# A two-unit attention start rewritten: scores two tiles ahead, probabilities of the second unit scaled before their transposes, and a last tile in two buffers

## The chip, the cores and the metric

The kernel runs on one NeuronCore of one Trainium2 chip. The metric is the time of one execution in microseconds. Each time is measured on the device; the median of three runs is compared. A profile is one more execution, in which every engine's instructions are recorded: TensorE (PE, with its weight loads as PEld), VectorE (DVE), ScalarE (ACT), GpSimd (POOL) and SyncE (SP), whose queue issues nearly all transfers.

## The reference

Windowed attention with sink tokens, then a two-layer MLP without gating. Four batches, eight heads, 768 positions, head width 64; then 3072 tokens through 512 x 2048 and 2048 x 512 weights.

```python
scores = scale * np.matmul(q, k.transpose(0, 1, 3, 2))
is_sink = pos[None, :] < int(n_sink)                     # n_sink = 4
in_window = (rel >= 0) & (rel < int(window))             # window = 128
scores = np.where(is_sink | in_window, scores, -1000000000.0)
scores = scores - np.max(scores, axis=-1, keepdims=True)
a = np.exp(scores)
a = a / (np.sum(a, axis=-1, keepdims=True) + 1e-09)
x = np.matmul(a, v)                                      # then heads side by side: (3072, 512)
h = x @ w_in
out = np.maximum(0.01 * h, h) @ w_out
```

The weights arrive as 64-bit floats and are decoded on the chip.

## The kernel before

The 3072 tokens are cut into eight units of 384 (half a batch each, three tiles of 128 queries). For each unit the attention gives `x` transposed, 512 x 384, in four pieces of two heads (a pair). Each piece is split into a rounded part `xh` and the rest `xl`. The MLP of a unit goes through 16 blocks of 128 hidden columns: 12 matmuls give `h` (L559; four pieces, three products each), ACT multiplies by 0.01 (L566), DVE takes the maximum `g` (L567), ACT rounds it to `gh` (L568), `gl` is the rest (L569: POOL in unit 0, DVE later), and nine matmuls (L580) add to three output banks. The nine output matmuls of a block are issued after the `h` matmuls of the next one. There is one bank for `h`, so the next block's `h` waits until `g` has been taken.

While PE runs the MLP of unit u, the attention of the next unit is put between: `attention_stream` yields after each small step and `mlp_stream` after each group of matmuls, and the loop at the end of `fast_path` decides by counts (`early_steps`, `LEAD0`, `LEAD`) how many attention steps are due. On PE this is the order of issue (`manual_schedule`). The other engines' order is put together by a scheduler when the program is built; on the chip each engine then works through its own list in order.

Units 0 and 1 are special (`u < EARLY`). They are computed in full precision, two heads at a time (`attend_pair`). For each of three tiles: scores of two heads (L283), on DVE mask and row minimum of the negated scores (L303), on ACT the exponential with its row sum (L305); later the transposes of the probabilities (L354, L355) and their copy by ACT to `pt` (L357, L360). POOL copies the sink columns to `sk`. After the third tile `sinks` transposes `sk` (L386) and multiplies it by `diag` (L390), and spreads the reciprocal row sums over 384 columns with POOL (L395, `rs`). Then `values_pair` multiplies by the values (L412, L414), transposes `rs` (L418), copies it back by ACT (L419), and DVE multiplies the accumulated values by it (L421, `xf`); `emit_x` makes `xh` (ACT, L515) and `xl` (DVE, L516). Since `rs` is one number for each query and head, this divides by the row sum after the values. Steps that aren't due yet wait in the list `pend`: a tile's transposes come one score tile later.

Before PE's first score tile there are 22 warm-up matmuls on zeros (L604), and on DVE and POOL the masks (`build_masks`): `m0`, `m1`, `m2` for one head's tile and from them the two 260 columns wide ones of units 0 and 1 (L137, L139). Weights: `load_weights` fetches 512 KB (L152, L153), DVE decodes in three operations (L172, L174, L176), ACT rounds (L180), POOL gives the rest (L181). A fetch waits either for the decode four blocks back or for a softmax some steps back (`PRED`); four blocks are fetched in the early stage, the others in the MLP of unit 0. At the end each output bank goes through a buffer of the ring `io` (two buffers) to HBM (L593, L594); the last tile is copied in two halves by ACT and DVE (L588, L590) into one buffer of another ring, `wraw`, and stored by two queues.

Of the kernel before, what the change touches and what calls it, by code (L numbers as in the profile page):

```python
# [20 lines left out]
P = 128  # L21
# [23 lines left out]
LEAD0 = 5  # L45
# [9 lines left out]
WARM = 22  # L55
DEPTH = 4
PRE0 = 5
PRED = 7
# [5 lines left out]
def build_masks(nc, cpool, tpool, lims):  # L64
    raw = tpool.tile([P, 2, 2], I32, name="lim_raw")
    words = lims.bitcast(I32).rearrange("(o w) -> o w", o=1)
    nc.sync.dma_start(out=raw.rearrange("p i w -> p (i w)"), in_=words.broadcast_to([P, 4]))
    lo = tpool.tile([P, 2], F32, name="lim_lo")
    hi = tpool.tile([P, 2], F32, name="lim_hi")
    lim = cpool.tile([P, 2], F32, name="lim")  # L70
    nc.vector.tensor_copy(out=lo, in_=raw[:, :, 0])
# [4 lines left out]

    rel = tpool.tile([P, 2 * P], F32, name="rel")
    key = tpool.tile([P, P], F32, name="key")
    nc.gpsimd.iota(rel, pattern=[[-1, 2 * P]], base=P, channel_multiplier=1,
                   allow_small_or_imprecise_dtypes=True)  # L80
    nc.gpsimd.iota(key, pattern=[[1, P]], base=0, channel_multiplier=0,
                   allow_small_or_imprecise_dtypes=True)
    cur = tpool.tile([P, P], F32, name="cur")
    prv = tpool.tile([P, P], F32, name="prv")
    m0 = cpool.tile([P, P], F32, name="m0")
    m1 = cpool.tile([P, WM], F32, name="m1")
    m2 = cpool.tile([P, WM], F32, name="m2")
    tri = cpool.tile([P, P], I8, name="tri")
    nc.vector.tensor_scalar(out=cur, in0=rel[:, P:], scalar1=0.0, scalar2=None, op0=ALU.is_ge)
    nc.vector.tensor_scalar(out=tri, in0=rel[:, P:], scalar1=0.0, scalar2=None, op0=ALU.is_lt)  # L90
    nc.vector.scalar_tensor_tensor(out=cur, in0=rel[:, P:], scalar=win, in1=cur, op0=ALU.is_lt, op1=ALU.mult)
    nc.vector.scalar_tensor_tensor(out=m0, in0=key, scalar=ns, in1=cur, op0=ALU.is_lt, op1=ALU.max)
# [19 lines left out]
def fast_path(ctx, tc, cpool, qp, qk, vu, vs, w_in, w_out, out, ident, wz, lim, masks, tri, diag, negm, wmin, wmax):  # L112
# [21 lines left out]
    for n, m in enumerate(masks[1:]):  # L134
        e = apool.tile([P, W3], F32, tag="stg", name=f"wide{n}")
        for sign, base, dst in ((1, -1, e[:, 0:P]), (-1, 0, e[:, WM:])):
            nc.gpsimd.affine_select(out=dst, in_=m[:, NSK:], pattern=[[sign, P]], base=base,  # L137
                                    channel_multiplier=-sign, compare_op=ALU.is_ge, fill=-MASKED)
# [688 lines left out]
```

## Time and profile before

| | |
|---|---|
| three runs | 714.91, 713.47, 716.59 us; median 714.91 us |
| profiled execution | 712.43 us, its span 710.7 us, mean granted clock of PE 0.995 |
| first score matmul on PE | 6.25 us |
| first `h` matmul (L559) | 41.20 us |
| last matmul's end | 703.5 us |

The page gives the span, the busy shares of each engine and the chain that ended last. Other views answer questions on the trace: who waited for whom, groups of instructions with their mean duration, the rows of one engine in time, and a table by stages with busy times and granted clock. Times in them are from the start of the span. "[1.31 <-DVE g L567]" behind a row is the idle time of its engine before it, and what ended it. A wait for several things is put down to the last.

### The profile page before, as it was taken

What the parts mean: (1) busy time and instruction counts of PE and PEld (TensorE: products, weight loads), DVE (VectorE), ACT (ScalarE), POOL (GpSimd) and SP (SyncE); (2) the same over time, 40 slices, a digit from 0 to 9 for tenths busy, and PEclk for the clock granted to TensorE, in tenths of its full rate; (3) what the DMA queues carried; (4) which work ended last, traced back from release to release, by engine and by line L of the source; (5) the groups of instructions that cost most, each with busy time, mean ns of one, the idle gap of its engine ahead of it and who ended that gap; (6) DMA issues with size and microseconds to landing.
All of it is one profiled execution on the core that took longest, in us unless ns stands there. A gap on an engine that the chain in (4) does not pass through costs nothing.

```text
span 710.7 us, 12473 instructions
## 1 busy us (share of the span) xinstructions
PE 692.1 (97%) x3871; PEld 602.9 (85%) x3871; DVE 533.9 (75%) x1717; ACT 417.8 (59%) x1162; POOL 397.4 (56%) x536
## 2 busy tenths in 40 slices
PE   8799999999999999999999999999999999999995
PEld 4467778999899899998989799989899998999884
DVE  6788989666678888888889888888888978642222
ACT  5766666576656666666665676666667566422221
POOL 2346668555557777667666777748666665400000
PEclk9999999999999999999999999999999999999999
DMA  6756654221124342243324433334332310000001
GB/s 189 262 171 227 204 170 167 67 74 56 54 70 139 125 127 92 96 155 117 101 97 132 127 123 108 99 106 144 103 100 98 102 54 30 0 19 28 1 0 50
DMA packets 42603, 74.32 MB, mean 105 GB/s; under 512 B 3489, under 2 KB 26273, under 8 KB 42529
## 3 DMA queue, kind: packets, MB, share of 16 engines
q1 hardware_dynamic: 42384, 73.31, 32.0%
q8 instruction: 33, 0.54, 0.3%
q14 instruction: 42, 0.34, 0.2%
q10 hardware_dynamic: 144, 0.13, 0.1%
HBM read 67.14 MB, written 6.29 MB: 103 GB/s over the span
## 4 chain that ended last, share of the span: by engine, by line
PE 89%; DVE 5%; ACT 2%; DMA 1%; issue 1%; POOL 1%; POOLq 0%; ACTq 0%; DVEq 0%
PE h L559 36%; PE o L580 36%; PE v L439 5%; PE s L291 4%; PE t L365 2%; PE v L412 1%; PE s L283 1%; DMA wiraw<-in_w_in 1%; PE v L414 1%; DVE gl L569 1%; DMA woraw<-in_w_out 1%; PE t L386 0%; PE t L433 0%; PE t L355 0%; PE t L418 0%
## 5 line engine op out<-in xcount | busy, mean ns | idle before, releaser
L559 PE MATMUL h<-xh,wi 128*128 128x384 f32 x1024 | 311.3, 352 | 1.7 <-DVE g L567 1.3
L580 PE MATMUL o<-wo,gh 128*128 128x512 f32 x768 | 247.1, 403 | 0.0
L559 PEld LDWEIGHTS h<-xh,wi 128*128 128x128 f32 x1024 | 190.0, 188 | 16.7 <-issue 2.5
L559 PE MATMUL h<-xl,wi 128*128 128x384 f32 x512 | 172.8, 337 | 0.0
L335 POOL TENSOR_SCALAR_AFFINE_SELECT pt<-stg 128x256 fp32r<-128x256 f32 x240 | 105.3, 463 | 95.1 <-DVE stg L373 71.5
L580 PE MATMUL o<-wo,gl 128*128 128x512 f32 x384 | 151.4, 394 | 0.0
L580 PEld LDWEIGHTS o<-wo,gh 128*128 128x128 f32 x768 | 132.3, 189 | 17.2 <-issue 0.7
L567 DVE TENSOR_TENSOR g<-h,g 128x384 f32<-128x384 f32 x128 | 71.0, 555 | 64.0 <-ACT g L566 63.0
L566 ACT ACTIVATE g<-h 128x384 f32<-128x384 f32 x128 | 62.4, 487 | 70.1 <-PE h L559 68.8
L559 PEld LDWEIGHTS h<-xl,wi 128*128 128x128 f32 x512 | 96.9, 189 | 3.0
L580 PEld LDWEIGHTS o<-wo,gl 128*128 128x128 f32 x384 | 72.1, 188 | 17.9 <-DVE gl L569 0.2
L568 ACT CAST gh<-g 128x384 fp32r<-128x384 f32 x128 | 65.5, 511 | 35.1 <-DVE g L567 32.6
L569 DVE TENSOR_TENSOR gl<-g,gh 128x384 fp32r<-128x384 f32 x112 | 76.4, 682 | 11.5 <-ACT gh L568 9.9
L320 ACT ACTIVATE pk<-pk,negm 128x128 f32<-128x128 f32 (+1 forms) x144 | 58.1, 404 | 37.8 <-DVE negm L317 37.2
L242 POOL TENSOR_TENSOR qksp<-qkraw,qksp 64x392 fp32r<-64x392 f32 (+1 forms) x48 | 58.5, 1219 | 25.9 <-ACT qksp L241 18.0
L291 PEld LDWEIGHTS s<-qksp 128*128 128x128 f32 x288 | 53.2, 188 | 9.3 <-issue 2.9
L372 ACT CAST stg<-t 128x128 fp32r<-128x128 f32 x120 | 31.0, 258 | 47.9 <-PE t L365 34.0
L291 PE MATMUL s<-qksp 128*128 128x260 f32 (+1 forms) x288 | 56.3, 277 | 2.4 <-DVE negm L317 2.4
L244 POOL TENSOR_TENSOR qksp<-qkraw,qksp 128x384 fp32r<-128x384 f32 x48 | 51.9, 1082 | 3.8
L326 DVE TENSOR_SCALAR pk<-pk,sm 128x132 f32<-128x132 f32 (+1 forms) x120 | 47.5, 396 | 2.1
L439 PEld LDWEIGHTS v<-pt,vsp 128*128 128x128 f32 x336 | 45.1, 189 | 2.7 <-DVE xf L445 0.6
L241 ACT CAST qksp<-qkraw 128x776 fp32r<-128x776 f32 (+1 forms) x48 | 42.9, 893 | 6.7 <-PE s L291 3.4
(132 smaller groups left out, 1058.8 us busy)
## 6 DMA issues: line engine op xcount, KB each, us to landing
qkraw<-in_qk SPq DMA_DIRECT2D x24, 454.0 KB, 3.3
qkraw<-in_qk SPq DMA_DIRECT2D x24, 388.0 KB, 3.6
wiraw<-in_w_in SPq DMA_DIRECT2D x16, 512.0 KB, 3.8
woraw<-in_w_out SPq DMA_DIRECT2D x16, 512.0 KB, 3.8
ciraw<-in_w_in SPq DMA_DIRECT2D x16, 512.0 KB, 3.7
coraw<-in_w_out SPq DMA_DIRECT2D x16, 512.0 KB, 3.5
out<-ob SPq DMA_DIRECT2D x23, 256.0 KB, 2.0
vraw<-in_vu SPq DMA_DIRECT2D x14, 256.0 KB, 2.6
```

The costliest lines, as they stand in the source:

```text
L242: nc.gpsimd.tensor_tensor(out=sp[D:P, TU:TU + n], in0=raw[D:P, TU:TU + n], in1=sp[D:P, TU:TU + n].bitcast(F32), op=ALU.subtract)
L244: nc.gpsimd.tensor_tensor(out=sp[:, TU + n:2 * TU + n], in0=raw[:, 0:TU], in1=sp[:, 0:TU].bitcast(F32), op=ALU.subtract)
L291: nc.tensor.matmul(ps[:, 0:kn], lhsT=sp[:, off + j * P:off + (j + 1) * P], rhs=sp[:, TU + k0:TU + k0 + kn], start=c == 0, stop=c == len(pa ...
L320: nc.scalar.activation(out=w, in_=w, func=AF.Exp, scale=-1.0, bias=neg, accum_out=sm)
L335: nc.gpsimd.affine_select(out=out, in_=src, pattern=([[0, x]] if x > 1 else []) + [[sign, P]], base=-1 if prev else 0, channel_multiplier= ...
L439: nc.tensor.matmul(out[:, o:o + m], lhsT=l, rhs=r, start=c == 0, stop=c == len(mms) - 1, skip_group_check=True)
L559: nc.tensor.matmul(ph[:, 0:TU], lhsT=w[:, cs], rhs=x, start=cc == 0 and c == 0, stop=cc == NCC - 1 and c == 2)
L566: nc.scalar.mul(g, ph[:, 0:TU], 0.01)
L567: anchor[0] = nc.vector.tensor_tensor(out=g, in0=ph[:, 0:TU], in1=g, op=ALU.max)
L568: nc.scalar.copy(out=gh, in_=g)
L569: (nc.gpsimd if u == 0 else nc.vector).tensor_tensor(out=gl, in0=g, in1=gh.bitcast(F32), op=ALU.subtract)
L580: nc.tensor.matmul(po[t], lhsT=gg[:, tsl], rhs=w, start=f == 0 and c == 0, stop=f == NFC - 1 and c == 2)
```

## The change

It has these parts. (1) `attend_pair` becomes `early_stream`, one stream over all 24 tiles of units 0 and 1: the scores of a tile are issued two tiles ahead of its transposes (`SAHEAD`), where it was one. The values of a pair follow the next score tile. Two pairs' values are loaded at the start, and the next load follows a `value` step. (2) In unit 1 each tile's row sums are made reciprocal at once, and ACT multiplies the probabilities by them (L477) before the transposes; `rs`, its transposes, its copies and the product `xf` stay in unit 0 alone, and `emit_x` reads the accumulated values of unit 1 from PSUM. (3) Two steps fewer come ahead of the MLP (`LEAD0`), and the early weight fetches have other distances. (4) 12 warm-up matmuls on zeros and four on another zero tile replace the 22; the masks are built wide first and folded for the later units. (5) The checks of the limits move late. (6) The last output tile's halves get a buffer each, one of `wraw` and one of `io`.

```diff
-LEAD0 = 5
+LEAD0 = 3
+SAHEAD = 2
-WARM = 22
+WARM = 12
+WARMR = 4
-PRE0 = 5
-PRED = 7
+PRE0 = 6
+PERIOD = 7
+PRED = 12
...
-        pace(dma, decoded[-DEPTH] if len(decoded) >= DEPTH else anchors[-PRED])
+        pace(dma, decoded[-DEPTH] if len(decoded) >= DEPTH else anchors[-min(PRED, len(anchors))])
...
     def values_pair(u, pair, state):
...
+        if u:
+            emit_x(u, pair, acc[:, 0:TU])
+            return
+        rs = state["rs"]
         fac = slot()
...
-    def attend_pair(u, pair, pend, state):
...
+    def early_stream(pend):
+        tiles = [(u, pair, j) for u in range(EARLY) for pair in range(NPAIR) for j in range(T)]
+        live = {}
+
+        def score(u, pair, j):
...
+            softmax_pair(u, pair, j, scores_pair(u, pair, j, st["raw"]), w, st["sm"])
+            sm = st["sm"][:, :, j] if u else st["sm"]
+            if u or j == T - 1:
+                nc.vector.tensor_scalar(out=sm, in0=sm, scalar1=1e-9, scalar2=None, op0=ALU.add)
+                nc.vector.reciprocal(out=sm, in_=sm)
+            if u:
+                for x in range(2):
+                    nc.scalar.mul(w[:, x, :], w[:, x, :], st["sm"][:, x, j:j + 1])
...
+        def value(u, pair):
+            values_pair(u, pair, live.pop((u, pair)))
+            n = u * NPAIR + pair + 2
+            if n < EARLY * NPAIR:
+                load_values(*divmod(n, NPAIR))
+
+        for k, tile_ in enumerate(tiles):
+            score(*tile_)
+            yield
+            while pend:
+                pend.pop(0)[1]()
+                yield
+            if k >= SAHEAD:
+                u, pair, j = tiles[k - SAHEAD]
+                turn(u, pair, j)
+                yield
+                if j == T - 1:
+                    gather(u, pair)
+                    yield
+                    pend.append((1, lambda u=u, pair=pair: value(u, pair)))
...
-                            nc.vector.tensor_copy(out=ob[:, 256:], in_=po[t][:, 256:])
-                            nc.sync.dma_start(out=out[r0:r0 + P, 256:], in_=ob[:, 256:])
+                            obs = [iopool.tile([P, 256], F32, tag=tag, name=f"ob{v}_{tag}", bufs=n)
+                                   for tag, n in (("wraw", 1), ("io", None))]
...
+                            nc.vector.tensor_copy(out=obs[1], in_=po[t][:, 256:])
+                            nc.sync.dma_start(out=out[r0:r0 + P, 256:], in_=obs[1])
...
+    for _ in range(WARMR):
+        nc.tensor.matmul(warm[:, 0:TU], lhsT=sts[1][:, 0:P], rhs=sts[1], start=True, stop=True)
...
-        if len(wts) < min(2 * PRE, (done - PRE0) // PRED):
+        if len(wts) < min(2 * PRE, (done - PRE0) // PERIOD):
             load_weights()
+    masks.extend(fold_masks(nc, cpool, wide))
```

Three places of the new order. The first is PE where unit 0's last pair ends and the MLP begins. In the names, `t` are transposes, `pe_p_j` the probabilities of pair p and tile j, `s` scores (two heads of a pair), `v_p` the values of pair p, `h_0` the first hidden block. Before, from the last pair's values on:

```order
L412 MATMUL v_3_560<-pt_3_427,vn_3_401 64x256 x4
...
L418 MATMUL t_568<-ident,rs_548 128x128 x3
L354 MATMUL t_579<-ident,pe_0_0_519 128x128
...
L283 MATMUL s_0_2_591<-qkn_0_332 128x260
...
L354 MATMUL t_601<-ident,pe_0_1_535 128x128
...
L559 MATMUL h_0_628<-xh_0_292,wi_322 128x384
```

On PE, at the same place, there stands now:

```order
L284 MATMUL s_0_2_530<-qkn_0_286 128x260
L284 MATMUL s_1_2_531<-qkn_0_286 128x260
L414 MATMUL v_3_552<-pt_3_391,vn_3_369 64x256 x4
L414 MATMUL v_3_552<-pt_3_391,vn_3_369 64x128 x2
L416 MATMUL v_3_552<-sn_3_525,vsraw_3_370 128x256
L424 MATMUL t_560<-ident,rs_527 128x128 x3
L587 MATMUL h_0_601<-xh_0_274,wi_307 128x384
...
L355 MATMUL t_611<-ident,pe_0_0_483 128x128
...
L587 MATMUL h_0_601<-xh_3_567,wi_307 128x384
```

The scores of unit 1's third tile moved ahead of the values of pair 3, and of unit 1's transposes the first tile's stand inside `h_0` and the second's behind it; between the reciprocals' transposes and the use of `xh_3` stand nine `h` matmuls and one tile's transposes.

The second is ACT at the same place, up to the rounding of the last piece of `x`. Before:

```order
L305 ACTIVATE pe_0_1_535,sm_0_517<-pe_0_1_535,negm 128x260 x2
L419 COPY rs_548<-t_568 128x384
L180 CAST wo_557<-wof_553 128x512
L357 COPY pt_0_518<-t_579 128x2x256
L515 CAST xh_3_575<-xf_3_573 128x384
```

On ACT there stands now:

```order
L306 ACTIVATE pe_0_1_503,sm_0_481<-pe_0_1_503,negm 128x260
L306 ACTIVATE pe_0_2_529,sm_0_481<-pe_0_2_529,negm 128x260
L477 ACTIVATE pe_0_0_483<-pe_0_0_483,sm_0_481 128x260 x2
L306 ACTIVATE pe_0_2_529,sm_0_481<-pe_0_2_529,negm 128x260
L477 ACTIVATE pe_0_1_503<-pe_0_1_503,sm_0_481 128x260 x2
L425 COPY rs_527<-t_560 128x384
L181 CAST wo_549<-wof_545 128x512
L477 ACTIVATE pe_0_2_529<-pe_0_2_529,sm_0_481 128x260 x2
L358 COPY pt_0_482<-t_611 128x2x256
L544 CAST xh_3_567<-xf_3_565 128x384
```

Two exponentials and six multiplications (L477) now stand ahead of `xh_3`.

The third is DVE at the end of the program, with what each row waits for (DMAHW4 and the like are the counters of eight transfers in turn). Before:

```order
L567 TENSOR_TENSOR g_15_9077<-h_15_9064,g_15_9077 128x384 [waits Activation_49]
L569 TENSOR_TENSOR gl_15_9079<-g_15_9077,gh_15_9078 128x384 [waits PE_49,Activation_49]
L593 COPY ob_0_9096<-o_0_8656 128x512 [waits DMAHW4_49,PE_49]
L593 COPY ob_1_9102<-o_1_8657 128x512 [waits DMAHW5_49,PE_49]
L590 COPY ob_2_9108<-o_2_8658 128x256 [waits DMAHW6_49,DMAHW1_49,DMAHW7_49,DMAHW0_49,Activation_49]
```

On DVE the program now ends:

```order
L595 TENSOR_TENSOR g_15_9058<-h_15_9045,g_15_9058 128x384 [waits Activation_49]
L597 TENSOR_TENSOR gl_15_9060<-g_15_9058,gh_15_9059 128x384 [waits PE_49,Activation_49]
L622 COPY ob_0_9077<-o_0_8637 128x512 [waits DMAHW4_49,PE_49]
L622 COPY ob_1_9083<-o_1_8638 128x512 [waits DMAHW5_49,PE_49]
L618 COPY ob_io<-o_2_8639 128x256 [waits DMAHW6_49,DVE_49,Activation_49]
```

The last copy now writes the buffer that `ob_0` of the same unit had, and waits for its transfer; before, it wrote the buffer that the late weight checks had used.

More of the change, by code (lines that the diff above doesn't have):

```diff
@@ L86, in build_masks @@
[L86 to L92, printed above, removed]
+    nc.vector.scalar_tensor_tensor(out=keep, in0=rel, scalar=win, in1=keep, op0=ALU.is_lt, op1=ALU.mult)
@@ L131, in fast_path @@
         sts.append(st)
-    wide = []
[L134 to L138, printed above, removed]
-        nc.gpsimd.tensor_copy(out=e[:, P:WM], in_=m[:, 0:NSK])
-        wide.append(e)
+    lim, m0, wide, tri, diag = build_masks(nc, cpool, mpool, iopool, apool, lims)
+    masks = [m0]
     xs = [[] for _ in range(NU)]
@@ L461, in pop @@
                 pend.pop(0)[1]()
                 yield
-        def gather():
-            state["st"] = sinks(u, pair, sk, state)
-        for j in range(T):
-            w = apool.tile([P, 2, W3], F32, tag="pk", name=f"pe{u}_{pair}_{j}", bufs=PKB)
-            softmax_pair(u, pair, j, scores_pair(u, pair, j, raw), w, sm)
-            if j == T - 1:
-                nc.vector.tensor_scalar(out=sm, in0=sm, scalar1=1e-9, scalar2=None, op0=ALU.add)
-                nc.vector.reciprocal(out=sm, in_=sm)
-            yield
-            yield from pop(3 if j else 1)
-            n = u * NPAIR + pair + 1
-            if j == 1 and n < EARLY * NPAIR:
-                load_values(*divmod(n, NPAIR))
-            pend.append((0, lambda j=j, w=w: tail_pair(u, pair, j, w, pt, sk)))
@@ L526, in attention_stream @@
         load_values(0, 0)
-        for u in range(EARLY):
-            for pair in range(NPAIR):
-                yield from attend_pair(u, pair, pend, state[pair % 2])
+        load_values(0, 1)
+        yield from early_stream(pend)
         for u in range(EARLY, NU):
@@ L624, in fast_path, with check_limits @@
             next(stream, None)
-    return flags[0]
-def needs_general(nc, pool, row, ident, lim, negm, wmin, wmax):
+    return flags[0], lim
+def check_limits(nc, pool, lim):
     bad = pool.tile([P, 6], F32, name="bad")
-    deep = pool.tile([P, 1], F32, name="deep")
     nc.vector.tensor_scalar(out=bad[:, 0:1], in0=lim[:, 0:1], scalar1=float(NSK), scalar2=None, op0=ALU.is_gt)
@@ L633, in needs_general @@
     nc.vector.tensor_scalar(out=bad[:, 2:3], in0=lim[:, 1:2], scalar1=float(P), scalar2=None, op0=ALU.is_gt)
+    return bad
+def needs_general(nc, pool, row, ident, bad, negm, wmin, wmax):
+    deep = pool.tile([P, 1], F32, name="deep")
     nc.vector.tensor_reduce(out=deep, in_=negm, axis=AX.X, op=ALU.max)
```

106 lines of the change are left out of this document (61 added, 45 removed).

## The prediction

> **What bounds the kernel now.** I read the page first: the busy shares, then the chain that ended last.
>
> ```profile
> span 710.7 us, 12473 instructions
> PE 692.1 (97%) x3871; PEld 602.9 (85%) x3871; DVE 533.9 (75%) x1717; ACT 417.8 (59%) x1162; POOL 397.4 (56%) x536
> PE 89%; DVE 5%; ACT 2%; DMA 1%; issue 1%; POOL 1%; POOLq 0%; ACTq 0%; DVEq 0%
> ```
>
> TensorE (PE) is busy 97% of the span and is 89% of the chain. An edit therefore moves the end only if it removes PE work, removes PE idle time, or lengthens the stretch after the last matmul. Next I read the waits of PE over the whole span (engine, line, who released it: sum, times, longest):
>
> ```profile
> PE t L354 <- ACT pe L305: 5.3, 5, 2.1
> PE s L291 <- DVE negm L317: 2.4, 2, 1.5
> PE h L559 <- DVE g L567: 1.3, 1, 1.3
> ```
>
> The largest wait, 5.3 us, is that of the probability transposes for the exponentials, and it belongs to the first two units, which the change rewrites. The table by stage shows where (columns: length, then busy time of PE, PEld, DVE, ACT, POOL, the granted clock, DMA share, GB/s):
>
> ```profile
> 0.00:6.25 6.25, 5.06 (x22) 2.52 (x22) 3.56 (x22) 1.28 (x1) 2.50 (x10) 1.00 0.60 168
> 6.25:41.20 34.95, 28.81 (x181) 15.92 (x181) 25.05 (x94) 24.78 (x81) 9.79 (x24) 0.95 0.65 211
> 41.20:45.70 4.50, 3.20 (x17) 2.28 (x16) 4.50 (x15) 3.67 (x11) 2.16 (x3) 1.00 0.74 244
> 45.70:110.00 64.30, 64.29 (x363) 50.74 (x364) 58.27 (x126) 40.73 (x98) 44.99 (x50) 1.00 0.64 206
> ```
>
> From 6.25 to 41.20 us, the attention of unit 0 before the first MLP matmul, no engine is full: PE idles 6.1 us, ACT 10.2, DVE 9.9. From 45.7 us on PE has no idle time, with DVE at 91% (58.27 of 64.30) and ACT at 63%. So there are three places to cost: the early stage, the dense stage behind it, and the end.
>
> **Part 1, the early stage (scores two tiles ahead, two values loads instead of one, earlier weights).** What ACT waits for in 6 to 45 us, grouped (mean ns of one, then idle before):
>
> ```profile
> L305 ACT ACTIVATE pe<-pe,negm 128x260 f32<-128x260 f32 x23 | 11.6, 507 | 1.7 <-DVE negm L303 1.6
> L515 ACT CAST xh<-xf 128x384 fp32r<-128x384 f32 x4 | 2.1, 515 | 2.1 <-DVE xf L421 2.1
> L419 ACT COPY rs<-t 128x384 f32<-128x384 f32 x4 | 1.9, 480 | 4.7 <-PE t L418 4.7
> L172 DVE TENSOR_SCALAR di<-wiraw 128x512 int32<-128x512 int32 x3 | 2.1, 692 | 2.0 <-DMA wiraw<-in_w_in 2.0
> ```
>
> ACT stands 4.7 us before the copies of the turned reciprocals, because in its fixed order nothing else is ready: the next tile's exponentials need scores that PE issues only after the values. With scores two tiles ahead, those exponentials stand in ACT's order before that copy, with their input already there. So the stage becomes limited by ACT's own work up to `xh3`, the last input of the first hidden tile (second order piece). That work is the 24.78 us of the table, plus what moves ahead of `xh3`: two exponentials of tile 2 of unit 1 and the six new multiplications. Their price:
>
> ```profile
> 7.18 0.40 ACT L305 ACTIVATE pe<-pe,negm 128x128 f32<-128x128 f32 x1 [5.10 <-DVE negm L303]
> 12.53 0.51 ACT L305 ACTIVATE pe<-pe,negm 128x260 f32<-128x260 f32 x1
> 12.95 0.19 ACT L305 ACTIVATION_READ_ACCUMULATOR pe<-pe,negm 128x1 f32 x1
> 13.04 0.50 ACT L305 ACTIVATE pe<-pe,negm 128x260 f32<-128x260 f32 x1
> ```
>
> An exponential takes 0.51 us start to start, 0.42 of it before its accumulator is read. A multiplication of the same size reads no accumulator, so I take 0.42. Added: 2 x 0.51 + 6 x 0.42 = 3.5, total 28.3 us. ACT begins at 7.18 us; I leave that start, though the shorter mask chain may gain some tenths. Without a gap `xh3` ends at 35.5 us; with all of the old 10.2 us of gaps, at 45.7. Going through ACT's rows in their new order with these durations, I find about 2 us of gaps (ACT still waits for the turned reciprocals of the first pair, and for DVE where a weight decode of 0.69 stands before a softmax). I take 2.0: `xh3` ends at 37.5, the last three hidden matmuls of `h0` at 38.4 (an estimate: `xl` on DVE and three matmuls behind it). DVE's own work stays below this: 25.05 plus three more decode steps of 0.69 from about 7 us is 34 us. The last rows of `h0` before:
>
> ```profile
> 40.83 0.27 PE L354 MATMUL t<-ident,pe 128*128 128x128 f32 x1
> 40.94 0.27 PE L355 MATMUL t<-ident,pe 128*128 128x128 f32 x1
> 42.96 0.71 PE L283 MATMUL s<-qkp 64*128 64x260 f32 x4
> 43.60 0.44 PE L559 MATMUL h<-xh,wi 128*128 128x384 f32 x1
> 44.06 0.34 PE L559 MATMUL h<-xh,wi 128*128 128x384 f32 x1
> 45.71 0.45 PE L559 MATMUL h<-xh,wi 128*128 128x384 f32 x1 [1.31 <-DVE g L567]
> ```
>
> Before, `h0` ends at 44.4, but by then PE has also done one score tile (42.96 to 43.60, 0.64) and one tile's four transposes (4 x 0.11) that now come later. So the fair comparison is 43.3 against 38.4: **4.9 us gained**, between 7 (no gap) and a loss of 3 (all gaps). The 1.31 us wait of `h1` for `g0` stays: in the new order too six `h1` matmuls stand directly behind `h0`.
>
> **Part 2, the clock.** While PE waited in the early stage its granted clock fell (a row of PE, then one-microsecond rows of the stage table, whose last column but two is the clock):
>
> ```profile
> 33.33 0.33 PE L354 MATMUL t<-ident,pe 128*128 128x128 f32 x1 [2.10 <-ACT pe L305]
> 32.00:33.00 1.00, 0.00 (x0) 0.00 (x0) 1.00 (x6) 1.00 (x3) 0.00 (x0) 1.00 0.63 232
> 34.00:35.00 1.00, 0.66 (x4) 0.49 (x6) 0.88 (x3) 1.00 (x5) 1.00 (x1) 0.88 0.85 245
> 35.00:36.00 1.00, 1.00 (x5) 0.30 (x3) 0.36 (x2) 0.75 (x3) 0.93 (x4) 0.50 0.66 231
> 37.00:38.00 1.00, 1.00 (x8) 0.52 (x6) 1.00 (x3) 0.65 (x4) 0.19 (x1) 0.50 0.00 0
> ```
>
> After 2.10 us idle and little work behind it the clock is 0.50 for some 3.2 us, 1.6 us lost; that loss lies inside the 44.4. Afterwards PE reaches `h0` at about 33 us, works 2 us, stands some 2 us for `xh3`, does three matmuls, and stands 1.3 us for `g0`: again over 3 of 4 us idle. I take one new drop, **1.6 us lost**; the bounds are 0 and 1.6. [...]
>
> **Part 3, the dense stage.** Four pairs of unit 1 lose three transposes each, with their copies on POOL and ACT and one product on DVE. On PE such a set holds its place for 0.30 us:
>
> ```profile
> 55.98 0.55 PE L418 MATMUL t<-ident,rs 128*128 128x128 f32 x3
> 56.28 0.71 PE L580 MATMUL o<-wo,gh 128*128 128x512 f32 x2
> ```
>
> PE is full there, so 4 x 0.30 = **1.2 us gained**. Against it 18 more multiplications (24 less the six above) come on ACT: 18 x 0.42 = 7.6 us, less four copies of 0.48. ACT goes from 63% to about 72%. ACT runs in order, and `g` (L594) and `gh` (L596) stand behind them; with `h` in a single bank, PE has the nine output matmuls, about 2.1 us, and what attention lies between to cover `g` on ACT and DVE. Bounds: 0, and 9 tiles x 0.84 = 7.6 if each pair of multiplications stands unhidden before a `g`. In most of ACT's rows they stand behind `g`, so I take **1.3 us lost**. DVE gains four products and gets 16 more operations on two columns; I cost that at zero, covered by its 9% of free time.
>
> **Part 4, the end.** The last output tile is split into two buffers. The VectorE half takes the ring `io` of two buffers, whose next one holds the first output tile of the last unit, so it must wait for that tile's transfer (third order piece). Before, it used a buffer that had long been free:
>
> ```profile
> 702.16 1.39 DVE L593 COPY ob<-o 128x512 f32<-128x512 f32 x2 [0.59 <-PE o L580]
> 702.88 1.86 SPq L594 DMA_DIRECT2D out<-ob  x2
> 703.97 0.42 DVE L590 COPY ob<-o 128x256 f32<-128x256 f32 x1 [0.41 <-ACT ob L588]
> 704.84 0.39 SPq L591 DMA_DIRECT2D out<-ob  x1
> out<-ob SPq DMA_DIRECT2D x2, 256.0 KB, 3.2
> out<-ob ACTq DMA_DIRECT2D x1, 128.0 KB, 2.2
> out<-ob SPq DMA_DIRECT2D x1, 128.0 KB, 3.0
> ```
>
> That transfer is issued at 702.88 and lands 3.2 us later, at 706.1. The copy moves from 703.97 to 706.1, its transfer starts at 706.6 and, now alone, takes 2.2 (the ACT half's) to 3.0: it lands at 708.8 to 709.6 instead of 704.84 + 3.0 = 707.84. What follows the last landing is unchanged. Bounds 0.9 and 1.8; I take **1.2 us lost**, nearer the lone transfer.
>
> **The sum.** 4.9 - 1.6 + 1.2 - 1.3 - 1.2 = 2.0 us gained. The profiled execution took 712.43 us (span 710.7), so 710.4 by its own time; the median of the three runs is 714.91, 2.5 us above it, so **712.9 us** on that scale.
>
> **The rivals.**
>
> *The clock holds.* No term of 1.6: 711.3. For it: PE's single gaps come out near 2 us, and the 1.31 us wait before `h1` started no drop. Against it: two gaps lie close together. Chance 0.22. [...]
>
> *All of it arrives.* Clock up, the multiplications hidden, ACT's gaps only 1 us: 5.9 + 1.2 - 1.2 = 5.9 gained, 709.0. For it: PE had no idle time at 91% DVE before, so the order carries much. Chance 0.20.
>
> *The lead does nothing.* ACT's gaps halve only, to 5.1: part 1 gives 1.8, and with the rest the sum is -1.1: 716.0. For it: the values still wait for the copies of the turned probabilities, which stand behind exponentials on ACT. Chance 0.12.
>
> *Slower, at the ACT queue before `g`.* If the multiplications stand unhidden, part 3 costs 7.6 instead of 1.3: sum -4.3, 719.2. It decides from the point where ACT's work per hidden tile fills PE's cover of about 2.1 us. Against it: ACT at 72%. Chance 0.08.
>
> **How the numbers follow.** The forecast holds 0.38. About 0.5% (3.6 us) is what a measurement of this kernel tells from no change: below 711.3 is faster, above 718.5 slower. Faster: 0.20, half of 0.22, and 0.04 of the forecast, 0.35. Slower: 0.08. The same: 0.57. The range goes from 708.0 to 717.5, which leaves out the slower case and the outer edge of the best one; the forecast's own is 711 to 715.
>
> **What would show it.** Right: the first `h` matmul near 33 us and `h1` near 39.7, against 41.20 and 45.71; the wait of the transposes for the exponentials mostly gone; a stretch of clock 0.50 near 38 us; 12 instead of 24 transposes of `rs`; in the dense stage `h` waiting for `g` about 1 us in sum; at the end the DVE copy released by a DMA 2 us later. Wrong: ACT with over 5 us of gaps before `xh3`, PE idle by more than 3 us in the dense stage, or a last copy that doesn't wait.

## The result and the profile after

| | before | after | ratio, 95% interval |
|---|---|---|---|
| first comparison (6 executions each) | 714.19 us | 710.63 us (710.07 to 712.19) | 0.9948, 0.9929 to 0.9968 |
| repeated later (15 and 10 executions) | 715.02 us | 711.49 us (710.46 to 712.03) | 0.9957, 0.9941 to 0.9973 |
| the profiled executions | 712.43 us, clock 0.995 | 712.19 us, clock 0.991 | |

The change makes the kernel faster by 0.4 to 0.5%, at the bound of what a measurement tells from no change. The prediction was 712.9 us (708.0 to 717.5). The executions of the kernel before fall into two groups of about equal size, 712.9 us (median) at a granted clock of 0.994 to 0.996 and 715.5 at 0.989 to 0.991 (with two exceptions), so its median shifts by one or two microseconds with the mix, and the two profiled executions alone (0.24 us apart) say little: that of before is among its quickest, that of after the slowest of six.

The page of the changed kernel first: busy shares and the chain that ended last.

```profile
span 710.5 us, 12455 instructions
PE 691.5 (97%) x3853; PEld 603.4 (85%) x3853; DVE 536.2 (75%) x1726; ACT 424.8 (60%) x1182; POOL 394.4 (56%) x531
PE 88%; DVE 6%; ACT 2%; issue 1%; DMA 1%; POOL 1%; DVEq 0%; ACTq 0%; POOLq 0%
```

TensorE is still the bound, with 18 matmuls fewer in the records. What it waits for has changed. From the waits of PE over the whole span (sum, times, longest):

```profile
PE s L292 <- DVE negm L318: 2.4, 2, 1.5
PE h L587 <- ACT xh L544: 1.6, 1, 1.6
PE h L587 <- DVE g L595: 1.3, 1, 1.3
PE t L387 <- POOL rs L396: 0.9, 1, 0.9
PE t L387 <- ACT pt L358: 0.8, 2, 0.4
PE o L608 <- POOL gl L597: 0.6, 1, 0.6
```

The 5.3 us that the transposes waited for exponentials are gone; new are one wait of 1.6 us for `xh3` and 1.7 us of the sinks' transposes (L387) in the early stage. The stage table, with the stages of the prediction and then three single microseconds (length, busy time of PE, PEld, DVE, ACT, POOL, granted clock, DMA share, GB/s):

```profile
6.25:41.20 34.95, 29.51 (x191) 17.48 (x188) 30.71 (x109) 30.10 (x95) 11.91 (x23) 0.97 0.78 256
41.20:45.70 4.50, 4.50 (x15) 3.40 (x15) 3.62 (x9) 2.18 (x6) 2.98 (x4) 0.50 0.65 218
45.70:110.00 64.30, 64.30 (x359) 50.49 (x358) 58.71 (x135) 47.43 (x115) 42.13 (x45) 1.00 0.62 201
39.00:40.00 1.00, 0.00 (x0) 0.00 (x0) 1.00 (x3) 0.76 (x2) 0.49 (x1) 0.67 0.94 333
45.00:46.00 1.00, 1.00 (x4) 0.93 (x3) 0.16 (x1) 0.97 (x4) 0.62 (x1) 0.50 0.50 134
46.00:47.00 1.00, 1.00 (x8) 0.83 (x6) 0.97 (x3) 0.35 (x2) 0.65 (x1) 0.91 0.93 328
```

In the early stage ACT went from 24.78 to 30.10 us of work in the same 35 us. In the dense stage PE stays full and ACT rises to 74%. From 39.3 to 46.2 us the clock is 0.50, 6.8 us in all; PE works through the last 6.1 of them, so some 3.0 us, half of these, are lost. The rows around the two waits, of ACT and PE:

```profile
35.81 0.92 ACT L477 ACTIVATE pe<-pe,sm 128x260 f32<-128x260 f32 x2
37.09 0.52 ACT L544 CAST xh<-xf 128x384 fp32r<-128x384 f32 x1
37.66 0.44 PE L587 MATMUL h<-xh,wi 128*128 128x384 f32 x1 [1.56 <-ACT xh L544]
40.12 0.69 PE L587 MATMUL h<-xh,wi 128*128 128x384 f32 x1 [1.25 <-DVE g L595]
```

`xh3` ends at 37.61 us (predicted 37.5), and `h1` starts at 40.12 (predicted near 39.7; 45.71 before). The last matmul of the program ends at 701.2 us against 703.5. The end of the program (rows of DVE and SP, then from the table of transfers the last store's time from issue to landing):

```profile
703.72 0.42 DVE L618 COPY ob_io<-o 128x256 f32<-128x256 f32 x1 [2.47 <-DMA out<-ob]
704.17 0.33 SPq L619 DMA_DIRECT2D out<-ob_io  x1
out<-ob_io SPq DMA_DIRECT2D x1, 128.0 KB, 2.5
```

The last copy waits 2.47 us for a transfer, as predicted. From the last matmul's end to the span's end are 9.3 us; before it was 7.2.

### The profile page after: what moved, and what is told of

It is laid out like the page before. It is cut to its first block, busy times and chain, and to the rows that moved or that the text cites. A ratio compares the mean times of both kernels' runs of the same rounds, so it can differ in the third digit from the quotient of the medians.

```text
span 710.5 us, 12455 instructions
## 1 busy us (share of the span) xinstructions
PE 691.5 (97%) x3853; PEld 603.4 (85%) x3853; DVE 536.2 (75%) x1726; ACT 424.8 (60%) x1182; POOL 394.4 (56%) x531
## 4 chain that ended last, share of the span: by engine, by line
PE 88%; DVE 6%; ACT 2%; issue 1%; DMA 1%; POOL 1%; DVEq 0%; ACTq 0%; POOLq 0%
PE h L587 36%; PE o L608 36%; PE v L445 5%; PE s L292 4%; PE t L366 2%; PE s L284 1%; PE v L414 1%; DVE gl L597 1%; DVE pe L304 1%; PE v L416 1%; PE t L387 0%; ACT pe L306 0%; PE t L439 0%; DMA lim_raw<-in_lims 0%; DMA out<-ob 0%
## 5 line engine op out<-in xcount | busy, mean ns | idle before, releaser
L310 DVE COPY_PREDICATED s<-tri,s 128x128 f32<-128x128 int8 x120 | 34.7, 289 | 18.2 <-PE s L292 17.2
```

## The experiments

Each was timed beside the kernel before. That kernel's median went from 713.5 to 715.0 us between these comparisons, about 0.002 of it, so smaller differences of ratio are read from the traces. Four marks of each trace carry the reading (us from the span's start; `h1` is the second hidden block's first matmul, "unit 0 out" the first copy of an output bank by DVE):

| kernel | h1 | unit 0 out | last matmul ends | span | median, ratio |
|---|---|---|---|---|---|
| before | 45.71 | 137.61 | 703.5 | 710.7 | |
| after | 40.12 | 135.06 | 701.2 | 710.5 | 710.63, 0.9948 |
| after, repeated | 40.03 | 135.10 | 701.2 | 709.7 | 711.49, 0.9957 |
| free last buffer | 40.12 | 134.97 | 701.1 | 708.9 | 709.52, 0.9935 |
| no scaling | 38.99 | 132.90 | 699.4 | 707.3 | 709.50, 0.9938 |
| gaps filled | 40.27 | 132.51 | 698.9 | 708.2 | 710.53, 0.9948 |
| free buffer, no scaling | 38.66 | 133.97 | 700.9 | 707.5 | 708.33, 0.9909 |
| free buffer, gaps filled | 40.24 | 132.46 | 698.8 | 706.4 | 707.59, 0.9901 |
| free buffer, late multiplications | 39.51 | 133.22 | 700.0 | 707.4 | 709.77, 0.9927 |
| scores one tile ahead | 41.81 | 134.68 | 701.4 | 709.8 | 711.78, 0.9968 |
| before, with scaling alone | 49.83 | 142.14 | 708.3 | 716.8 | 716.56, 1.0034 |
| free buffer, no scaling, filled | 38.88 | 133.22 | 699.7 | 706.9 | 708.46, 0.9923 |
| the same, pairs 1 to 3 scaled | 38.68 | 130.28 | 695.3 | 702.0 | 703.98, 0.9865 |

From "unit 0 out" to the last matmul's end all take 565 to 567 us (before 565.9): what the change does, it does in the first 140 us and behind the last matmul.

### The last buffer

```diff
-                            obs = [iopool.tile([P, 256], F32, tag=tag, name=f"ob{v}_{tag}", bufs=n)
-                                   for tag, n in (("wraw", 1), ("io", None))]
+                            obs = [iopool.tile([P, 256], F32, tag="wraw", name=f"ob{v}_wraw", bufs=1),
+                                   mpool.tile([P, TU], F32, tag="g", name=f"ob{v}_g")[:, 0:256]]
```

> The changed kernel, but the VectorE half of the last output tile goes to a buffer that has long been free, so that it waits for no transfer. The copy should start right after the ACT half (0.4 us behind it, not 2.5). In both profiles the span ends 6.3 to 6.4 us behind the end of this copy (704.39 to 710.7 before, 704.14 to 710.5 in the changed kernel), so if the end hangs on DVE's queue, the stretch from the last matmul's end to the span's end shrinks from 9.3 to 7.2 us and the time by 2.1 us, to about 708.5 at the median. Rival: the end hangs on the last transfer's landing (706.7 in the changed kernel); then 1.2 us at most. Second rival: the wait is covered by another transfer that lands as late; then nothing.

Rows of DVE and SP at the end, and the last store:

```profile
701.55 0.42 DVE L618 COPY ob_g<-o 128x256 f32<-128x256 f32 x1 [0.41 <-ACT ob_wraw L616]
702.58 0.39 SPq L619 DMA_DIRECT2D out<-ob_g  x1
out<-ob_g SPq DMA_DIRECT2D x1, 128.0 KB, 3.8
```

The copy starts 2.2 us earlier, its store only 1.6 (SP is still issuing the two before it), and the store takes 3.8 us instead of 2.5, so that it lands at 706.4 against 706.7. Ratio 0.9935 (0.9912 to 0.9958). From the last matmul's end to the span's end, the five profiles with the waiting copy (after, its repetition, no scaling, gaps filled, one tile ahead) have 9.3, 8.5, 7.9, 9.3 and 8.4 us, mean 8.7; the six with the free buffer have 7.8, 6.6, 7.6, 7.4, 7.2 and 6.7, mean 7.2. So the wait costs about 1.5 us, between the 2.1 of the theory and the 1.2 of the rival. About half of it, 0.7 us, lies before the last store lands (5.4 us behind the last matmul's end on the mean of the five, 4.7 on that of the six); what takes the rest, behind the landing, no row shows. The stretch varies by up to 1.4 us among kernels that end with the same code, and the kernel before with scaling alone, whose copy doesn't wait either, has 8.5 where the kernel before has 7.2. So one pair of profiles doesn't give the price, and with these two counted it is 1.3.

### The scaling, taken out

Unit 1 then divides after the values, as unit 0 does (`rs` made, turned and multiplied in both units, the multiplications on ACT gone):

```diff
-        if u == 0:
-            state["rs"] = xpool.tile([P, TU], F32, tag="xf", name=f"rs{pair}")
+        if u < EARLY:
+            state["rs"] = xpool.tile([P, TU], F32, tag="xf", name=f"rs{u}_{pair}")
...
-        if u:
-            emit_x(u, pair, acc[:, 0:TU])
-            return
...
-            if u:
-                for x in range(2):
-                    nc.scalar.mul(w[:, x, :], w[:, x, :], st["sm"][:, x, j:j + 1])
```

> The changed kernel, but unit 1 divides after the values as unit 0 does (reciprocals turned on PE, copied, multiplied by DVE), with no multiplication of probabilities on ACT. Theory: in the early stage the six multiplications (2.5 us on ACT ahead of xh3) are gone, so PE's gap of 1.56 us before the last matmuls of h0 shrinks to under 0.5 and h1 starts 1 to 2 us earlier than 40.1; in the dense stage it costs 4 x 0.30 = 1.2 us of PE again and saves the 0.6 us wait for gl. In sum within 1.5 us of the changed kernel. Rival: the scaling on ACT carries the gain; then about 2 us or more slower than the changed kernel and near the kernel before.

ACT's `xh3` and PE's start of `h1`:

```profile
35.46 0.52 ACT L538 CAST xh<-xf 128x384 fp32r<-128x384 f32 x1
38.99 0.45 PE L581 MATMUL h<-xh,wi 128*128 128x384 f32 x1 [1.18 <-DVE g L589]
```

`xh3` starts 1.63 us earlier without the six multiplications, `h1` 1.13. PE's wait of 1.56 us for `xh3` is gone, and one of 0.73 for `xl` has taken its place. Ratio 0.9938 (0.9916 to 0.9959): the rival, that the scaling carries the gain, fell. The same with the free buffer:

> The changed kernel without the scaling on ScalarE (unit 1 divides after the values, as unit 0 does) and with the free buffer for the last half tile. Theory (in the early stage the six multiplications delay xh3 by 1.6 us and bring the clock drop, in the dense stage the scaling saves 1.2 us of transposes; the last half tile's wait costs 1.1): xh3 at 35.5 us, no stretch at 0.50, the last matmul ends near 699.4 us as with the scaling alone taken out, the VectorE copy no longer waits (idle 0.4 us before it), and the time is 1.5 to 2.5 us under the changed kernel's, the best of all. Rival (the scaling pays for itself in the dense stage and the end is set by something behind the last copy): within 0.7 us of the changed kernel's.

Ratio 0.9909 (0.9886 to 0.9931), 3.2 us under the changed kernel on the same chip, more than the 1.5 to 2.5 expected; about half of it is the buffer, by the mean above. The trace did what was expected except for the clock, and with the drop the last matmul ends at 700.9 us instead of 699.4. One-microsecond rows of the run without scaling, then of this one, whose PE has the same two gaps (0.73 and 1.17 us):

```profile
39.00:40.00 1.00, 1.00 (x6) 1.00 (x6) 0.96 (x2) 0.54 (x2) 0.80 (x1) 1.00 0.25 62
40.00:41.00 1.00, 1.00 (x7) 0.42 (x7) 0.90 (x3) 0.00 (x0) 1.00 (x2) 1.00 0.95 313
...
39.00:40.00 1.00, 1.00 (x8) 0.69 (x6) 0.90 (x2) 0.20 (x1) 1.00 (x1) 0.89 0.47 121
40.00:41.00 1.00, 1.00 (x5) 0.47 (x4) 0.69 (x1) 0.24 (x1) 1.00 (x2) 0.50 1.01 359
```

The one keeps its clock, the other is at 0.50 for 3.4 us. The same gaps were followed by a drop in one execution and by none in the other.

### The gaps, filled

Matmuls on zeros go into an output bank not yet in use, nine ahead of `h0`'s last piece and seven ahead of `h1`:

```diff
+    def filler(n):
+        fl = ps_o.tile([P, 512], F32, tag="o1", name="fill")
+        for _ in range(n):
+            nc.tensor.matmul(fl[:, 0:TU], lhsT=wz[:, 0:P], rhs=wz, start=True, stop=True)
...
+                    if u == 0 and fc == 0 and cc == NCC - 1:
+                        filler(9)
+                    if u == 0 and fc == 1 and cc == 0:
+                        filler(7)
```

> The changed kernel with 9 and 7 matmuls on zeros added on PE into a free bank, in the two gaps before the last matmuls of h0 and before h1 (about 0.16 us each). Theory: the gaps cause the stretch at clock 0.50 from 39.4 to 46.1 us; with them filled the clock stays at 1.0 and h1 starts where it did or up to 0.3 us later; against an execution with the long drop 3 us are gained, against the changed kernel's median about 1 to 1.5 us: 709 to 709.7. Rival: the drop has another cause or matmuls on zeros don't count; then the clock still falls to 0.50 near 39 us and the time is that of the changed kernel or up to 0.3 us more.

> The changed kernel with the free buffer for the last half tile and with 16 matmuls on zeros in TensorE's two gaps before the last three matmuls of h0 and before h1 (they go into an output bank that is not yet in use). Theory (the two gaps of 1.56 and 1.25 us start the clock drop, which costs 0 to 3.3 us by execution): granted clock 1.00 from 30 to 60 us in every profile, the last matmul ends near 698.9 us, and the time is 1.5 to 3 us under the changed kernel's. Rival (while the clock is at 0.50 TensorE would wait for ScalarE and VectorE anyway, so a held clock brings little): clock held, but the time is only the 1.1 us of the free buffer lower.

PE's rows of the fillers, and a row of the stage table, all of the second of these runs:

```profile
36.05 1.63 PE L574 MATMUL fill<-wz 128*128 128x384 bf16 x9
38.84 1.31 PE L574 MATMUL fill<-wz 128*128 128x384 bf16 x7
40.00:41.00 1.00, 0.92 (x5) 0.77 (x5) 0.96 (x3) 0.78 (x2) 0.56 (x1) 1.00 0.48 142
```

The clock holds at 1.00 in both profiles (their mean granted clock is 0.996, against 0.991 and 0.992 in the two of the changed kernel), `h1` starts 0.1 us later for the fillers, and "unit 0 out" comes 2.6 us earlier than in the two profiles of the changed kernel. These work 6.1 and 6.4 us at half clock, which makes 3.0 and 3.2; the later `h1` takes 0.1, and 0.3 to 0.5 I can't place. In time the first run disagrees with its trace: 710.53 us, 0.9948 (0.9926 to 0.9969), no gain where 709 to 709.7 us were expected. The second, with the buffer, has 0.9901 (0.9878 to 0.9923), 3.9 us under the changed kernel on its chip. If the buffer accounts for about 1.5 of these, 2.4 are left for the clock, near the 2.6 of the traces. But the runs with the buffer alone and the fillers alone took only 1.1 and 0.1 us less than the changed kernel's first median, so the traces show this division and the times don't. Why the first did not show it in time stays open; its stretch behind the last matmul was as long as the changed kernel's, 9.3 us.

### The multiplications, later

Tiles 1 and 2 of pair 0 of unit 1 are multiplied only behind `xh3`:

```diff
+            if u and pair == 0 and j:
+                with tc.issue_after(rounded[-1].ins):
+                    scale(u, pair, j)
```

> The changed kernel, but the multiplications of tiles 1 and 2 of unit 1's first pair are put behind the rounding of xh3 in ACT's order (4 x 0.42 = 1.7 us less ahead of it; the copy of the turned probabilities also goes behind it). Theory: ACT's work ahead of xh3 sets the end of the early stage, so xh3 is rounded 1.5 to 2 us earlier than 37.09 us, PE's 1.56 us gap goes to under 0.3, h1 starts near 38.5 instead of 40.12, and the clock drop becomes rarer; 1.5 to 2.5 us less than the changed kernel. Rival: xh3 waits for DVE (xf and the decodes ahead of it), not for ACT; then it starts within 0.5 us of where it did.

It has no trace that can be read beside the others and gives only a time: 709.61 us, 0.9939 (0.9915 to 0.9963), 1.0 us under the changed kernel's first median where 1.5 to 2.5 were expected. With the free buffer:

> The changed kernel with the free buffer for the last half tile, and with the multiplications of tiles 1 and 2 of unit 1's first pair put behind the rounding of xh3 in ScalarE's order. Theory (ScalarE's queue sets xh3): xh3 starts 0.8 to 1.6 us before the 37.09 us of the changed kernel, the first gap of TensorE (1.56 us) falls under 0.8, h1 starts near 39.3, and the clock drop is gone or shorter; time 1.5 to 2.5 us under the changed kernel's. Rival (what waits behind these multiplications, the transposes of those tiles, becomes late instead): xh3 earlier, but a new wait of TensorE for the multiplied probabilities of 0.8 us or more behind h1, and the time lower by the 1.1 us of the buffer alone.

ACT's `xh3`, its multiplications and `g` of `h0`, then `h1` on PE:

```profile
35.80 0.51 ACT L553 CAST xh<-xf 128x384 fp32r<-128x384 f32 x1 [0.63 <-DVE xf L428]
36.70 1.72 ACT L481 ACTIVATE pe<-pe,sm 128x260 f32<-128x260 f32 x4
38.32 0.47 ACT L603 ACTIVATE g<-h 128x384 f32<-128x384 f32 x1
39.51 0.44 PE L596 MATMUL h<-xh,wi 128*128 128x384 f32 x1 [1.90 <-DVE g L604]
```

`xh3` starts 1.29 us earlier and PE's wait for it falls from 1.56 to 0.34 us, as the theory has it: ACT's queue sets `xh3`, until at 35.80 DVE's `xf` does. But the four multiplications now stand ahead of `g`, and `h1` waits 1.90 us instead of 1.25. `h1` gains 0.6 us, and a drop of one 3.4 us stretch remains. Ratio 0.9927 (0.9904 to 0.9951), 1.7 us under the changed kernel on this chip, of which the buffer can carry most. The rival's wait for the multiplied probabilities did not come; what came late was `g`, which the prediction's slower rival names.

### The changed kernel again

> The changed kernel once more, unedited, as the measure for the three others on this chip. If its gain of 3.6 us was no accident of the earlier runs: 0.993 to 0.997 of the kernel before. If TensorE's clock drop behind 39 us differs from execution to execution (as the granted clocks 0.991 to 0.997 of its earlier executions suggest), this profile may show none, one or two stretches at 0.50; with none, the last matmul ends 1.5 to 3.3 us before the 701.22 us of the first profile, and the times of its executions spread over 2 us again.

The profile again is at 0.50 for 6.8 us (39.6 to 46.4); the granted clocks of its ten executions go from 0.991 to 0.995.

### Scores one tile ahead

```diff
-SAHEAD = 2
+SAHEAD = 1
```

> The changed kernel with the scores one tile ahead of the transposes (SAHEAD = 1), everything else as changed. Theory (the lead of two tiles carries the early gain of 4.5 us): ScalarE's idle time before the copies of the turned reciprocals comes back (3 to 5 us in all), TensorE waits again for the exponentials (3 us or more before the first h), h1 starts at 43.5 to 46 us instead of 40.1, and the time is 2 to 4.5 us above the changed kernel's (711 to 715). Rival (the second values load, the earlier weights and masks carry it): h1 before 42 us and the time within 1 us of the changed kernel's.

From the waits of PE up to 140 us, ACT's wait for the turned reciprocals up to 41 us, PE's start of `h1`, and DVE's decode of the weight block in question:

```profile
PE t L355 <- ACT pe L306: 2.9, 5, 1.0
...
ACT rs L425 <- PE t L424: 1.3, 3, 0.7
...
41.81 0.45 PE L587 MATMUL h<-xh,wi 128*128 128x384 f32 x1 [1.71 <-DVE g L595]
...
27.14 0.68 DVE L173 TENSOR_SCALAR di<-wiraw 128x512 int32<-128x512 int32 x1
```

The rival holds on `h1` (before 42 us), though the time, 711.78 us (0.9968, 0.9954 to 0.9982), is 1.1 above the changed kernel's in the first comparison. PE has done the same attention work ahead of `h1` as in the changed kernel (15 score tiles, up to the third of unit 1, and the transposes of unit 1's first tile), so `h1` compares as 41.81 against 40.12, and the second tile of lead is worth 1.7 us. The other 2.8 of the 4.5 us come without it. Nor does ACT's idle time before the turned reciprocals come back, as the theory has it: 4.7 us before, it is 1.3 here and 0.7 in the changed kernel. Where the 2.8 may come from, the trace of the kernel before shows at the same decode (rows of DVE and SP):

```profile
24.12 0.38 SPq L152 DMA_DIRECT2D wiraw<-in_w_in  x1
...
29.86 0.69 DVE L172 TENSOR_SCALAR di<-wiraw 128x512 int32<-128x512 int32 x1 [2.00 <-DMA wiraw<-in_w_in]
...
31.66 0.42 DVE L303 CUSTOM_DVE_ANT_0 pe<-s,wide 128x260 f32<-128x260 f32 x1
```

DVE stood 2.00 us for a weight block that SP had issued at 24.12 us, and the softmax of the next tile stood behind it. Its exponentials are those for which PE waited 2.10 us at 33.33, and from 34.8 to 38.2 us followed the half clock, 1.7 us lost. 2.0 and 1.7 make 3.7, more than the 2.8, so the two are enough, but how much of each reached `h1` isn't shown. With one tile of lead the fetch is issued at 19.69 us (changed kernel 20.19), the decode starts at 27.14 without a wait, and the clock stays at 1.00 (0.998 on the mean of the execution, 0.995 in the kernel before). Which of the new distances of the fetches, the second values load and the place of the values brings the earlier issue, no run separates.

### The scaling alone

```diff
-        if u < EARLY:
+        if u < EARLY and u == 0:
...
+            smj = sm[:, :, j] if u else sm
+            if u or j == T - 1:
+                nc.vector.tensor_scalar(out=smj, in0=smj, scalar1=1e-9, scalar2=None, op0=ALU.add)
+                nc.vector.reciprocal(out=smj, in_=smj)
+            if u:
+                for x in range(2):
+                    nc.scalar.mul(w[:, x, :], w[:, x, :], sm[:, x, j:j + 1])
```

> The kernel before with only the scaling on ScalarE in unit 1. Theory (scaling is worth 1.7 us in the dense stage, as the stretch from h1 to unit 0's end was 92.2 us with it and 93.9 without it where the clock held; and the early stage does not suffer here, since ScalarE had 4.7 us of gaps): h1 within 1 us of 45.71, unit 0's first output copy 1 to 2 us ahead of the 137.61 of the kernel before, ratio 0.997 to 0.999. The prediction on record (1.2 gained, 1.3 lost): ratio 1.000. Rival (multiplications stand before g and hold it): waits of h for g of 1 us or more in the dense stage, ratio above 1.001.

It is slower: 1.0034 (1.0016 to 1.0053). Rows of ACT, DVE and PE behind `h0`:

```profile
47.32 0.92 ACT L481 ACTIVATE pe<-pe,sm 128x260 f32<-128x260 f32 x2 [0.23 <-DVE sm L478]
48.14 0.47 ACT L575 ACTIVATE g<-h 128x384 f32<-128x384 f32 x1
48.62 0.69 DVE L176 SCALAR_TENSOR_TENSOR wof<-woraw,do 128x512 int32<-128x512 int32 x1
49.22 0.55 DVE L576 TENSOR_TENSOR g<-h,g 128x384 f32<-128x384 f32 x1
49.83 0.44 PE L568 MATMUL h<-xh,wi 128*128 128x384 f32 x1 [2.81 <-DVE g L576]
```

The multiplications need a reciprocal per tile from DVE, where weight decodes of 0.69 us stand before it; they start at 47.32 and hold `g` on ACT until 48.14, and then a decode holds it on DVE until 49.22. PE waits 2.81 us instead of 1.31. So my theory fell and the rival's wait is real, though at the border and not in the dense stage: it came once, and up to 140 us `h` doesn't wait for `g` again. It costs 1.5 us, and the dense stage gains nearly as much: from `h1` to "unit 0 out" are 92.3 us with 1.7 lost to a half-clock stretch behind the wait, so 90.6 against 91.9 before, 1.3 less. The other 2.6 us by which `h1` is late lie ahead of `h0`. There the first exponential on ACT starts 1.0 us later than before, and two half-clock stretches (26.7 to 30.1 and 36.9 to 43.7 us) lose 5.1 us instead of 1.7. Both begin before the first multiplication (38.46 us), the first behind a wait of 1.86 us. So the time says that this kernel is slower, but its trace doesn't show that the scaling makes it so; why stays open.

### Scaling where it costs nothing

Two runs with the free buffer and ten filler matmuls (four ahead of the `xl` matmul of `h0`'s last piece, six ahead of `h1`): one without scaling, one with pairs 1 to 3 of unit 1 scaled and pair 0 divided after the values:

```diff
+                    if u == 0 and fc == 1 and cc == 0:
+                        filler(6)
...
+                        if u == 0 and fc == 0 and cc == NCC - 1 and c == 1:
+                            filler(4)
...
-        if u == 0:
+        if (u, pair) <= (1, 0):
...
-        if u:
+        if (u, pair) > (1, 0):
             emit_x(u, pair, acc[:, 0:TU])
...
+            scaled = (u, pair) > (1, 0)
...
-            if u:
+            if scaled:
                 for x in range(2):
```

(The lines on `(u, pair)` are those of the second run; the first has the edit of the run without scaling in their place.)

> The changed kernel without the scaling, with the free buffer for the last half tile, and with ten matmuls on zeros in the two gaps that are left (four before the xl matmul of h0's last piece, six before h1). Theory (without scaling h1 is 1.2 us earlier and the dense stage 1.7 us longer, so with a held clock the scaling is worth about 0.5): clock 1.00 behind 36 us, h1 near 38.8, unit 0's first output copy near 132.7, time 0.2 to 0.8 us above that of the kernel with scaling, fillers and free buffer (707.6 on another chip). Rival (scaling costs more than it brings): unit 0's first output copy before 132.0 and the time under 707.

> As the run beside it without scaling (free buffer, ten matmuls on zeros), but with pairs 1 to 3 of unit 1 scaled on ScalarE; only pair 0, whose multiplications stand ahead of xh3, divides after the values. Theory (the early cost of the scaling is that of pair 0 alone, and three of four parts of the dense gain stay): h1 near 38.8 us, unit 0's first output copy at 131.0 to 131.8, the time 0.7 to 1.5 us under that of the run without scaling: the fastest of all. Rival (pair 1's multiplications now come where g is late): waits of h for g of 0.8 us or more between 40 and 60 us, and no gain over the run without scaling.

Without scaling: 708.46 us, 0.9923 (0.9907 to 0.9939). With pairs 1 to 3: **703.98 us, 0.9865 (0.9843 to 0.9887)**, the best of all, 10.5 us under the kernel before. Its `h1` on PE, and the only row of PE's waits from 39 to 131 us:

```profile
38.68 0.45 PE L597 MATMUL h<-xh,wi 128*128 128x384 f32 x1 [0.19 <-DVE g L605]
...
PE h L597 <- DVE g L605: 0.2, 1, 0.2
```

From `h1` to "unit 0 out": 94.3 us without scaling, 92.2 with all four pairs (fillers, free buffer), 91.6 with three. Of the 2.7 us between the first and the last, 0.9 are three sets of transposes at 0.30, 0.8 a wait of `o` for POOL's `gl` that vanished, 0.2 a wait of the values; 0.8 I can't place. "Unit 0 out" is thus 2.9 us earlier, at 130.28 instead of the 131.0 to 131.8 expected, and the time is 4.5 us lower instead of 0.7 to 1.5. Another 1.5 us of its lead arise at 400 us, by an accident that the last section shows.

## Why the prediction was right, and where not

The forecast said 2.0 us gained and the comparisons give 3.5. The sign and the range hold, and in its steps the likeliest case was the right one: most of the early gain arrives, and part goes to a new drop of the clock and to the end. The number owes something to luck. 710.63 lies just below the 711 to 715 that the forecast kept for itself, and nearest to the rival in which the clock holds (711.3), which did not occur. The 2.5 us added to 710.4 came from a median of three, and the 3.5 depend on the executions of the kernel before: against the 712.9 of its one group the changed kernel's two medians are 1.4 to 2.3 us lower, against the 715.5 of the other 4.0 to 4.9. No trace shows an execution of the second group, so what takes its time stays open. The terms, by the profiled executions:

| term | predicted | measured |
|---|---|---|
| early stage, up to `h1` | +4.9 | +4.5 (45.71 to 40.12, less 1.1 of attention not yet done) |
| clock | -1.6 | -2.7 in the profile (its stretch from `h1` to "unit 0 out", 94.9, against 92.2 with the gaps filled) |
| dense stage | +1.2 - 1.3 | +0.8 (91.9 and the 1.1, against 92.2) |
| end | -1.2 | -2.1 between the two profiles, -1.5 over eleven |

The measured terms sum to +0.5; the two profiled executions differ by 0.24, and the stretch from "unit 0 out" to the last matmul, 0.25 longer after, holds the difference. Errors of 0.4 to 1.1 us in each term, of both signs, went into it.

**Part 1** has the right size and, for a good part, the wrong cause. ACT's work in its new order, taken as 28.3 us with 2.0 us of gaps, came to 28.1 and 2.4, so that `xh3` ended at 37.61 us (37.5 predicted), and a multiplication takes 0.40 us start to start (0.42). But the step "with scores two tiles ahead, those exponentials stand in ACT's order before that copy" carries 1.7 us of the 4.5: with one tile of lead, most of ACT's wait before that copy is gone already. The other 2.8 came with the rest of the new early stage, where DVE no longer stands for a weight block and the half-clock stretch behind it is gone; how they divide is argued above, not shown. The row of that wait (2.0 us, `di`) stood in the prediction's own list; I read it as ACT's idle time and did not follow what stood behind it on DVE.

**Part 2** named the two gaps that lie close together, and they are 1.56 and 1.25 us. The term was sized as one stretch of some 3.2 us; in both profiles of the changed kernel it was twice as long. The first comparison's four executions with a higher granted clock than the profiled one's 0.991 took 710.1 to 710.7 us, so that median may carry less of this loss than the profile; the repetition's ten, at 0.991 to 0.995, show no such order.

**Part 3** had the right gain (1.2; the stretches with and without scaling differ by 1.3 and 2.1) and a loss in the wrong place. "1.3 us lost" for multiplications ahead of `g` in the dense stage did not come: PE waits there only 0.6 us, for `gl`, and over the whole stage the change gains 0.8. The multiplications that cost are the six before `xh3` (1.1 us of `h1`). The slower rival's mechanism is real, as the run with scaling alone shows, but it strikes at the border of attention and MLP, where `g` has no output matmuls to cover it, not through 110 us.

**Part 4** was right in mechanism: the copy waits for the transfer of the ring's buffer, and is 2.1 us later against the last matmul. Its store lands 1.1 us later against the last matmul in the two profiles (5.4 against 4.3), near the 1.2 predicted. The step "what follows the last landing is unchanged" did not hold there: 3.8 us follow it, against 2.9. In all the price is 1.5 over eleven profiles.

**The rivals.** "The lead does nothing" is near on the cause (the second tile of lead is worth 1.7 us, and it leaves 1.8 for all of part 1), but not on the time, since the other early parts carry the rest of the gain. "The clock holds" did not occur in the changed kernel's profiles; with fillers it gives 2.6 us to "unit 0 out". "All of it arrives" would need that and the free buffer: the run with both has 707.59 us.

## To other kernels

A wait in an in-order queue is to be followed to what stands behind it on that queue: here DVE's 2.0 us for a weight block came out on PE as a wait for ACT. An operation moved to a queue with free time still costs where that queue is the last to release a stage, here 1.1 us of `h1`; put it on those tiles whose results are not next, here pairs 1 to 3 and not pair 0. A buffer for the last store belongs in a ring that no transfer still holds: here the copy waited 2.47 us for one, and 0.41 without.

## What the runs showed of the hardware

**The half-clock stretches were 3.4 us long or twice that.** Read from the clock's rows, they are 3.4 us (before, 34.8 to 38.2; the run with late multiplications and the free buffer; the run without scaling and with the free buffer; two in the run with scaling alone) or 6.8 (after 39.3 to 46.2, its repetition 39.6 to 46.4, the free-buffer run 39.2 to 46.0, one in the run with scaling alone), and the same gaps of 0.73 and 1.17 us led to one in one execution and to none in another. Nor did the length of a gap alone decide it: a drop followed 1.56 and 1.25 us with three matmuls between them, and none a single gap of 1.65 us in the kernel before; single gaps of 2.10 us there and of 1.86 in the run with scaling alone were followed by one. What sets the two lengths, and what decides whether a stretch comes, no run here shows.

**One DVE operation took three times its time where POOL was at work.** It is the place of the 1.5 us that the best kernel gains at 400 us. The wait of PE, DVE's row before it and POOL's at the same time, in the changed kernel:

```profile
398.05 1.64 DVE L597 TENSOR_TENSOR gl<-g,gh 128x384 fp32r<-128x384 f32 x1
...
397.99 1.28 POOL L257 TENSOR_TENSOR vsp<-vraw,vsp 128x512 fp32r<-128x512 f32 x1
...
400.51 0.48 PE L292 MATMUL s<-qksp 128*128 128x260 f32 x2 [1.51 <-DVE negm L318]
```

`gl` takes 0.56 us at the median. Here it begins 0.06 us behind POOL's operation, ends 0.4 behind that one's end, and the scores' softmax minimum behind it on DVE makes PE wait 1.51 us. The kernel before has this meeting at this place too (`gl` 1.65 us); `gl` takes 1.63 to 1.65 us there also in the repetition and in the runs with scaling alone, with late multiplications, with buffer and fillers, and in both with the free buffer and no scaling. In the best kernel POOL's operation comes at another moment against DVE's rows:

```profile
392.37 0.56 DVE L607 TENSOR_TENSOR gl<-g,gh 128x384 fp32r<-128x384 f32 x1
393.98 1.45 DVE L546 TENSOR_TENSOR xl<-xf,xh 128x384 fp32r<-128x384 f32 x1 [0.17 <-ACT xh L545]
...
393.72 1.29 POOL L257 TENSOR_TENSOR vsp<-vraw,vsp 128x512 fp32r<-128x512 f32 x1
```

Now `xl` is drawn out instead (1.45 us; its median in the changed kernel is 0.72), and nobody waits for it. Both operations end 0.42 us behind POOL's (399.69 against 399.27 us, 395.43 against 395.01); what draws them out beside POOL's operation, no run here shows. The gain was not planned, and was seen in the one trace of that kernel.
